# An attention and gated feed-forward kernel: six loads and adds per batch in place of eight accumulating ones

## The chip, the core and the metric

The kernel runs on one core of one Trainium2 chip. The metric is the device time of one execution in microseconds (us), the median of several runs. In the text PE is the engine of the matrix products, DVE the vector engine, ACT the scalar engine, POOL the GpSimd engine, SP the engine that issues most of the DMAs. Each engine works through its own list of instructions in a fixed order and waits where an operand is not ready.

## The reference

Keys and values are averaged over groups of 8 positions, so 576 queries of each of 8 batches and 8 heads meet 72 pooled keys and values; then comes a gated feed-forward layer.

```python
k_p = k.reshape(B, H, Sp, pool, D).mean(axis=3)      # B=8 H=8 S=576 Sp=72 D=64
v_p = v.reshape(B, H, Sp, pool, D).mean(axis=3)
scores = scale * q @ k_p.T; attn = softmax(scores)
x = (attn @ v_p)  # to 4608 rows of 512
g = x @ w_gate                                       # 512 -> 1536
out = (g / (1 + exp(-g)) * (x @ w_val)) @ w_out      # 1536 -> 512
```

All inputs and outputs are float32. The kernel splits each float32 operand into two 16-bit parts and adds up three products, which keeps the precision.

## The kernel before, in words

The 4608 rows of x are nine tiles of 512. A tile is filled by pieces of up to 128 queries, 40 pieces in all, 5 of each batch. A piece (the function `answer`) goes: scores on PE (L578), maximum and subtraction on DVE (L587, L588), exponential on ACT, a high part on ACT (L649) and a low part on POOL (L654, L655), a DMA transpose by SP into the tile `pt` (L1198), products with the values on PE (L663 to L666 for batches 0 and 1, L673 to L679 for batches 2 to 7), division on DVE (L683), a low part of x on POOL (L1315) and, for batches 2 to 7, one more DMA transpose by SP into x (L1319).

The feed-forward layer of a tile is 12 steps, one for each chunk of 128 hidden units. A plain step is 24 products of 512 columns (L775 to L777). A fast step does the same by a scheme of seven half-size products: 42 products of 256 columns (L879), with two additions on DVE (L942, L947); it needs weights that were converted on DVE, POOL and ACT (L800, L806, L812, L819) and sums of x (L840 to L848). Tiles 0 and 1 use plain steps. The gate's end is L723 (ACT) and L726 (DVE), the value's end L731 (DVE), and the result is stored to DRAM (`hd`, L903). From about 737 us on the product with w_out runs (L1565 to L1580).

The weights come as chunks in 64-bit form and are decoded on DVE, ACT and POOL (L335 to L389); the 12 chunks of w_out are loaded and decoded likewise (L330, then L335 and L358 with 512 columns) and stored back to DRAM (L395).

Batches 0 and 1 pool their keys and values on DVE, POOL and PE (L400 to L407, L501). For batches 2 to 7 the host only lays keys and values out as eight parts of 128 x 864 numbers, the eight positions of a group; they are added up while they are loaded: SP loads the first part (L1159), and POOL issues seven DMAs that accumulate onto it (L1161), each after the one before has landed. The sum lies in a buffer called box, one for even and one for odd batches. Then `prep` takes its maximum on DVE (L459), sums it over the rows on PE (L303, L304), scales, and spreads the result on ACT, DVE and POOL (L469 to L481).

What stands in each engine's list, and in which order, is decided at build time by the class Order: a planner in which every piece of work is a generator that asks for buffers, for flags, or for an engine with an assumed duration; the planner always takes what can begin first and, among what can begin nearly at once, the lowest rank. Buffers are handed out from pools: `mid` (3 buffers), `load` (3 tokens for bulk loads of SP), PSUM banks `gate`, `val`, `att`, `vs`. An assumed duration in the source is a number for this planner and not a measurement. A changed duration, pool or rank moves instructions on all engines.

Of the kernel before, what the change touches and what calls it, by code (L numbers as in the profile page):

```python
# [17 lines left out]
P = 128  # L18
POOLW = 8
# [42 lines left out]
class Order:  # L62
# [40 lines left out]
    def flag(self, name):  # L103
        return "flag", name
# [85 lines left out]
def attention_then_swiglu(  # L190
# [90 lines left out]
    )  # L281
    zeros = hp.tile([P, TILE // 2], F32, name="zeros", tag="rs0", bufs=1).bitcast(F16)

# [8 lines left out]
    def fields():  # L292
        nc.gpsimd.memset(zeros, 0.0)
        for i in range(2):
            nc.gpsimd.memset(halves[i][:, 2 * NJ * P :], 0.0)
            nc.gpsimd.memset(vst_h[i], 0.0)
            nc.gpsimd.memset(vst_l[i], 0.0)
# [459 lines left out]
    def f_room(name):  # L757
# [234 lines left out]
    def chunk(c):  # L992
# [25 lines left out]
        tj = t  # L1018
        t = yield op("ACT", 1640, lambda: w_sums(c), tj)
        where, t0 = yield get("att")  # L1020
        t = yield op("PE", 300, lambda: w_total(c, where), t, t0)
        t = yield op("DVE", 350, lambda: w_scale(c), t)
        put("att", where, t)
        order.start(("early", u + 0.01), factors(c, t))
        for i in range(2):
            th = yield op("ACT", 716, lambda: w_high(c, i), t)
            tl = yield op("DVE", 690 + 0 * i, lambda: w_low(c, i), th)
            order.done(("decoded", c, i), tl)

    def factors(c, t):  # L1030
        t = yield op("POOL", 450, lambda: nc.gpsimd.tensor_mul(p2w[:, c, 2:3], p2w[:, c, 0:1], p2w[:, c, 1:2]), t)
# [4 lines left out]
        t = yield op("POOL", 450, lambda: nc.gpsimd.tensor_mul(un_of[0][:, c], p2w[:, c], xs[0]["mt"]), t)  # L1036
        order.done(("un", c), t)
# [37 lines left out]
    def keys(b, g):  # L1075
        if b:
            n, t0 = yield get("mid")
            t = yield bulk(576, lambda: k_load(b, g, n), t0)
            t = yield op("POOL", 2900, lambda: k_sum(b, g), t)
            put("mid", n, t)  # L1080
        else:
            if not g:
                where, t0 = yield get("ws")
            t = yield bulk(576, lambda: k_load(b, g), 0)
            if g:
                tp = yield op("POOL", 1500, k_last, t)
                t = yield op("DVE", 1190, lambda: k_sum(b, g), t)
                t = max(t, tp)
                t = max(t, (yield flag(("keys", 0, 0))))
                spent.append((raw, "raw"))  # L1090
                put("ws", (raw, "raw"), t)
            else:
                t = yield op("DVE", 2210, lambda: k_sum(b, g), t)
        order.done(("keys", b, g), t)

    def pooled_values(b):
# [15 lines left out]
        order.done(("scaled", b), t)  # L1112
        order.start(("early", (0.32, SECOND + 0.32)[b]), left_values(b, t))
# [3 lines left out]
        put(("gate", "val")[b], where, max(t, tl[0]))  # L1117
        order.done(("values", b), max(t, tl[1]))
# [6 lines left out]
    def values_in(b, g, where, t0):  # L1125
# [3 lines left out]
        t = yield bulk(512, lambda: v_load(b, g, n), tm)  # L1129
        t = yield op("PE", 1850, lambda: v_sum(b, g, where), t, t0)  # L1130
        if n is not None:
# [21 lines left out]

    def kv_sums(b, t):
        box(0)
        box(1)
        o = home["kv", b % 2]
        src = kv[b - SPLIT]
        t = yield bulk(400, lambda: nc.sync.dma_start(out=o, in_=src[0]), t)  # L1159
        for n in range(1, POOLW):  # L1160
            t = KV_LAND + (yield op("POOL", 900, lambda: nc.gpsimd.dma_start(out=o, in_=src[n], accum_op=ALU.add), t))  # L1161
        order.done(("kv", b), t)

    def prep(b):

        split = yield flag("boxes")
        if b > SPLIT + 1:
            split = yield flag(("split", b - 2))
        order.start(("kv", b), kv_sums(b, split))
        t = yield flag(("kv", b))  # L1170
        mx = small.tile([P, 1], F32, name="mx1")
# [6 lines left out]

        t = yield op("PE", 300, total, t, t0)
        t = yield op("DVE", 350, lambda: pow2_above(p2s[:, b, 2:3], inv[:, b, 2:3], sums_of["ps"]), t)  # L1180
# [19 lines left out]
    def tile_x(i):  # L1200
# [10 lines left out]

        t = yield op("DVE", 900, rates, t)
        order.done(("rate", i), max(t, t0))
# [11 lines left out]
    def answer(t):  # L1225
# [15 lines left out]
        for g in range(2):  # L1241
            homes[g], t1 = yield get("att")
            t0 = max(t0, t1)
        tp = yield op("PE", 750, lambda: ps.update(scores(b, s0, m, homes)), ta, t0)
        put("qt", t["qt"], tp)
# [5 lines left out]
        if old:  # L1251
# [6 lines left out]
            if t["n"] in ON_POOL:  # L1258
                tp = yield op("POOL", 1560, lambda: normalise(nc.gpsimd, m, sc, t["ri"]), tp)
# [4 lines left out]
            tp = yield op("ACT", 1100, lambda: soft_high(m, sc, half), tp, th)  # L1264
            tp = yield op("POOL", 1700, lambda: soft_low(m, sc, half), tp)
            put("sc", s, tp)
# [13 lines left out]
        if not old:  # L1280
# [4 lines left out]

            te = max(tr, (yield op("DVE", 1030, ratios, te)))
        where, t0 = yield get("att")
        ps = {}
        x = xs[i]
        if old:  # L1290
# [8 lines left out]
            tp = yield op("DVE", 750, lambda: x_low(ps["o"], m, x, off, r), tp)  # L1299
            put("att", where, tp)  # L1300
        else:
# [8 lines left out]
            tp = yield op("DVE", 750, lambda: divided(o, ps["o"], m, t["ri"], r), tp, te)  # L1310
            put("att", where, tp)
            n, t0 = yield get("xt")
# [16 lines left out]
        if not left_of["b", b]:  # L1329
            order.done(("batch", b), tp)  # L1330

    wpart = {}
# [124 lines left out]
    def cut_operand(p, k, src, t):  # L1457
# [3 lines left out]
        for n in range(3):  # L1461
            th = yield op("ACT", 1043, lambda: nc.scalar.copy(rows[n], src[:, 2 * n : 2 * n + 2]), t, t0)  # L1462
            eng, ns, on = (("POOL", 2500, nc.gpsimd), ("DVE", 2000, nc.vector))[n == 2]
            tl = yield op(
# [200 lines left out]
    def all_lines():  # L1665

        home["ws"] = const.tile([P, 3 * 3 * DM // 2], F32, name="mixed", tag="wo_l", bufs=1)
        order.free["DVE"], order.free["POOL"] = 3300, 2400
        order.done("start", 0)

        def first_fields():
            order.done("fields", (yield op("POOL", 2800, fields, 0)))
# [4 lines left out]
        order.start(("early", 0.3), pooled_values(0))  # L1677
        for c in range(NCH):
# [102 lines left out]
```

## Time and profile before

| what | value |
|---|---|
| median of 3 runs | 1008.36 us (1005.07 to 1016.50) |
| profiled execution, its own time | 1008.69 us |
| span from its first to its last instruction | 1006.9 us |
| PE busy | 904.1 us, 90% of the span |
| DVE, ACT, POOL busy | 715.7, 474.5, 509.3 us |
| DMA queue of POOL (accumulating) | 18.58 MB, 12.5% of 16 engines' span |
| DMA queue of SP | 126.84 MB, 45.6% |

The profile is one execution; times in it count from the span's start. A wait is an engine's idle time before an instruction and is put down to what ended it. PE's matmuls overlap, so PE can be called busy while it waits a little; what PE needs at full pace is read from the number of products in a stretch in which it never waits.

### The profile page before, as it was taken

The numbers are of one execution on the slowest core, as the hardware profiler recorded it, in microseconds if no ns is written. First come the engines' busy times: TensorE is split into PE (matmuls) and PEld (weight loads), VectorE is DVE, ScalarE is ACT, GpSimd is POOL, SyncE is SP. The second block draws the span as 40 slices with busy tenths as digits, with TensorE's granted clock in tenths as the row PEclk, the third lists the DMA queues.
The fourth block names the chain that finished last, engine by engine and source line by source line (L and its number), as shares of the span: only waits on it lengthen the run. The fifth ranks groups of instructions, "written<-read, shape, count | busy, mean of one in ns | idle before, by whom it ended". The sixth has DMA issues, their size and how long they took to land. (4 is left out here: it accounts for less than half of the span.)

```text
span 1006.9 us, 17492 instructions
## 1 busy us (share of the span) xinstructions
PE 904.1 (90%) x6708; PEld 641.7 (64%) x6730; DVE 715.7 (71%) x1095; ACT 474.5 (47%) x821; POOL 509.3 (51%) x437
## 2 busy tenths in 40 slices
PE   5579887768699898899999999999999899999998
PEld 4566443333367577688878888888855455555554
DVE  7878693672889788888686765547754959687791
ACT  3776652331354465556454444446544344354442
POOL 2542462554465497636342421203355767778692
PEclk9588997998799999999999999999999999999999
DMA  8935997999888878855445241123653080625301
GB/s 287 303 103 170 237 189 142 191 159 154 140 168 178 155 171 186 187 131 131 93 108 118 70 101 62 61 66 127 220 219 105 8 306 21 253 81 190 145 22 63
DMA packets 136148, 146.54 MB, mean 146 GB/s; under 512 B 81792, under 2 KB 102272, under 8 KB 133760
## 3 DMA queue, kind: packets, MB, share of 16 engines
q1 hardware_dynamic: 130016, 126.84, 45.6%
q0 software_dynamic: 6048, 18.58, 12.5%
q8 instruction: 53, 0.87, 0.4%
q14 instruction: 31, 0.25, 0.1%
HBM read 86.51 MB, written 40.89 MB: 127 GB/s over the span
## 5 line engine op out<-in xcount | busy, mean ns | idle before, releaser
L1579 PE MATMUL ps<-low,wsh 128*128 128x512 bf16 x384 | 146.2, 381 | 5.7 <-DVE low L1466 4.1
L879 PEld LDWEIGHTS <-mixed 128*128 128x128 f16 x1404 | 136.4, 98 | 20.3 <-issue 2.1
L879 PEld LDWEIGHTS <-wgv_h 128*128 128x128 f16 x1248 | 121.0, 98 | 35.6 <-issue 17.1
L723 ACT ACTIVATE hf<-ps,un 128x512 f32<-128x512 f32 (+1 forms) x112 | 75.0, 670 | 104.9 <-PE ps L879 61.8
L879 PE MATMUL ps<-xc,mixed 128*128 128x256 f16 x936 | 123.2, 274 | 0.9 <-ACT ps L939 0.9
L879 PE MATMUL ps<-xc,wgv_h 128*128 128x256 f16 x624 | 110.7, 274 | 14.7 <-DVE ps L947 12.7
L726 DVE SCALAR_TENSOR_TENSOR hf<-hf,ps 128x512 f32<-128x512 f32 (+1 forms) x112 | 74.2, 663 | 64.6 <-ACT hf L723 64.2
L731 DVE SCALAR_TENSOR_TENSOR hf<-ps,un,hf 128x512 f32<-128x512 f32 (+1 forms) x112 | 81.4, 727 | 49.6 <-PE ps L879 28.6
L879 PE MATMUL ps<-x,wgv_h 128*128 128x256 f16 x624 | 109.2, 273 | 0.0
L776 PE MATMUL ps<-x,wgv_h 128*128 128x512 f16 (+1 forms) x272 | 101.7, 374 | 1.2 <-DVE x L693 1.2
L777 PE MATMUL ps<-x,wgv_l 128*128 128x512 f16 (+1 forms) x272 | 101.3, 373 | 1.3 <-DVE wgv_l L389 1.3
L775 PE MATMUL ps<-x,wgv_h 128*128 128x512 f16 (+1 forms) x272 | 102.5, 377 | 0.0
L879 PE MATMUL ps<-xc,wgv_l 128*128 128x256 f16 x312 | 85.6, 274 | 0.0
L879 PE MATMUL ps<-x,wgv_l 128*128 128x256 f16 x312 | 85.0, 273 | 0.0
L1579 PEld LDWEIGHTS <-wsh 128*128 128x128 bf16 x384 | 37.5, 98 | 50.9 <-issue 9.5
L1161 POOL DMA_DIRECT2D box<-kv_parts x42 | 37.1, 899 | 63.0 <-DMA box<-kv_parts 61.2
L1466 POOL TENSOR_TENSOR low<-wgv_h,hs 128x1024 bf16<-128x1024 f32 x18 | 51.2, 2868 | 33.7 <-ACT hs L1462 33.7
L1315 POOL TENSOR_TENSOR box<-sc,box 128x512 f16<-128x512 f32 (+1 forms) x30 | 38.5, 1284 | 54.4 <-ACT box L1314 54.4
L879 PEld LDWEIGHTS <-wgv_l 128*128 128x128 f16 x624 | 61.2, 98 | 7.4
L879 PE MATMUL ps<-x,mixed 128*128 128x256 f16 x468 | 64.5, 274 | 0.5 <-DVE ps L942 0.5
L654 POOL TENSOR_TENSOR half<-sc,half 128x448 f16<-128x448 f32 (+1 forms) x30 | 33.4, 1114 | 55.8 <-ACT half L649 55.6
L844 POOL TENSOR_TENSOR fx<-fx 128x256 f32<-128x256 f32 x40 | 29.6, 740 | 60.1 <-DVE fx L840 57.8
(181 smaller groups left out, 2101.4 us busy)
## 6 DMA issues: line engine op xcount, KB each, us to landing
hd<-hf SPq DMA_DIRECT2D x104, 256.0 KB, 2.4
ws<-w_all SPq DMA_DIRECT2D x36, 512.0 KB, 6.0
box<-kv_parts POOLq DMA_DIRECT2D x42, 432.0 KB, 7.7
wgv_h<-hd SPq DMA_DIRECT2D x9, 1536.0 KB, 6.8
wgv_l<-hd SPq DMA_DIRECT2D x9, 1536.0 KB, 8.9
out_t<-ob SPq DMA_DIRECT2D x36, 256.0 KB, 4.1
qt<-q_rows SPq DMA_DIRECT2D x32, 256.0 KB, 3.9
wd<-wf SPq DMA_DIRECT2D x12, 256.0 KB, 4.3
```

Of the source, the lines that this page charges most:

```text
L654: nc.gpsimd.tensor_sub(a[:, :, SP:], sc[:n, :, : P - SP], a[:, :, : P - SP])
L723: nc.scalar.activation(hf, gate, AF.Tanh, scale=un[:, c, 0:1])
L726: nc.vector.scalar_tensor_tensor(out=hf, in0=hf, scalar=1.0, in1=gate, op0=ALU.add, op1=ALU.mult)
L731: nc.vector.scalar_tensor_tensor(out=out, in0=val, scalar=un[:, c, 2:3], in1=hf, op0=ALU.mult, op1=ALU.mult)
L775: nc.tensor.matmul(o, wh, x["h"][:, j, a:e], start=(j == 0), stop=False)
L776: nc.tensor.matmul(o, wh, x["l"][:, j, a:e], start=False, stop=False)
L777: nc.tensor.matmul(o, wl, x["h"][:, j, a:e], start=False, stop=(j == NJ - 1))
L879: nc.tensor.matmul(o, a, b, start=begin and j + n == 0, stop=j == HJ - 1 and n == 2, skip_group_check=True,)
L1161: t = KV_LAND + (yield op("POOL", 900, lambda: nc.gpsimd.dma_start(out=o, in_=src[n], accum_op=ALU.add), t))
L1315: tp = yield op("POOL", 1205, lambda: nc.gpsimd.tensor_sub(xt[:, DM:], o, xt[:, :DM]), tp)
L1466: lambda: on.tensor_sub(low[:, 2 * n : 2 * n + 2], src[:, 2 * n : 2 * n + 2], rows[n].bitcast(F32)),
L1579: nc.tensor.matmul(o, top, where[1][:, c], start=False, stop=False, skip_group_check=True)
```

## The change

It has four parts.

1. Keys and values of batches 2 to 7: the accumulating DMAs go. A batch is loaded in six parts, each with all eight positions of 144 of the 864 columns (128 x 8 x 144, 576 KB, one contiguous row of 4608 bytes in each partition). SP issues the load into a buffer of `mid`, and POOL adds the eight up with three additions (576, 288 and 144 numbers a partition) into box. 6 loads and 42 accumulating DMAs become 36 loads and 36 groups of three additions.
2. PSUM: the products of values for batches 0 and 1 get a bank of their own (`wv`, formerly one of two banks of `val`), and both banks of `vs` go to `val` later; after batch 1 the bank `wv` is lent to `gate`.
3. The rank of the first values (0.9 in place of 0.3) and the assumed durations of several operations change, and the first operations stand in another order.
4. A buffer of zeros that nothing reads is no longer cleared.

```diff
-KV_LAND = 5500
+BANKS = "val", "val"
+VALUES = 0.9
+LENT = "gate"
...
-            "gate": [(ps_gv, "gv0"), acc[0]], "val": [(ps_gv, "gv1"), acc[1]], "vs": [acc[2], acc[3]],
+            "gate": [(ps_gv, "gv0"), acc[0]], "val": [(ps_gv, "gv1")], "wv": [acc[1]], "vs": [acc[2], acc[3]],
...
-    def kv_sums(b, t):
-        o = home["kv", b % 2]
-        src = kv[b - SPLIT]
-        t = yield bulk(400, lambda: nc.sync.dma_start(out=o, in_=src[0]), t)
-        for n in range(1, POOLW):
-            t = KV_LAND + (yield op("POOL", 900, lambda: nc.gpsimd.dma_start(out=o, in_=src[n], accum_op=ALU.add), t))
-        order.done(("kv", b), t)
+    def kv_part(b, c, ready):
+        n, t0 = yield get("mid")
+        _, t1 = yield get("load")
+        part = {}
+        def load():
+            part["in"] = buffer(mid, [P, POOLW, KV // 6], F32, "in", "mid", at=n)
+            nc.sync.dma_start(out=part["in"], in_=kv[b - SPLIT, c])
+        t = yield bulk(576, load, t0, t1)
+        cs = slice(c * KV // 6, (c + 1) * KV // 6)
+        dst = home["kv", b % 2][:, cs]
+        def add():
+            a = part["in"]
+            nc.gpsimd.tensor_add(a[:, :4], a[:, :4], a[:, 4:])
+            nc.gpsimd.tensor_add(a[:, :2], a[:, :2], a[:, 2:4])
+            nc.gpsimd.tensor_add(dst, a[:, 0], a[:, 1])
+        t = yield op("POOL", 2800, add, t, ready)
+        put("mid", n, t)
+        order.done(("kv", b, c), t)
...
-            order.start(("early", (0.31, SECOND + 0.3)[b] + 0.01 * g), values_in(b, g, where, max(t, tb)))
+            order.start(("early", (VALUES, SECOND + 0.3)[b] + 0.01 * g), values_in(b, g, where, max(t, tb)))
...
-        where, t0 = yield get("att")
+        where, t0 = yield get("wv" if old else "att")
...
+            if b == SPLIT - 1:
+                where, t0 = yield get("wv")
+                put(LENT, where, t0)
...
+    kv = kv.reshape(B - SPLIT, POOLW, P, 6, -1).transpose(0, 3, 2, 1, 4)
```

The first place is POOL's list where batches 2 and 3 are spread (L473) and the first low parts of their weights are made (L654, L655). Before, it reads (box is the buffer with the sums, fw a buffer for converted weights, half the low parts of a piece):

```order
L473 TENSOR_TENSOR box<-box,masks 128x512 x2
L1161 DMA box<-kv_parts 128x864
L654 TENSOR_TENSOR half_135<-sc,half_135 128x8x56
L655 TENSOR_TENSOR half_135<-sc,half_135 128x128
L806 TENSOR_TENSOR fw<-fw 128x256 x2
L1161 DMA box<-kv_parts 128x864 x2
L806 TENSOR_TENSOR fw<-fw 128x256 x2
L654 TENSOR_TENSOR half_136<-sc,half_136 128x8x56
L655 TENSOR_TENSOR half_136<-sc,half_136 128x128
```

Now it reads (in is the loaded part):

```order
L473 TENSOR_TENSOR box<-box,masks 128x512
L1169 TENSOR_TENSOR in<-in 128x576
L1170 TENSOR_TENSOR in<-in 128x288
L1171 TENSOR_TENSOR box<-in 128x144
L1169 TENSOR_TENSOR in<-in 128x576
L1170 TENSOR_TENSOR in<-in 128x288
L1171 TENSOR_TENSOR box<-in 128x144
L654 TENSOR_TENSOR half_135<-sc,half_135 128x8x56
L655 TENSOR_TENSOR half_135<-sc,half_135 128x128
L1169 TENSOR_TENSOR in<-in 128x576
L1170 TENSOR_TENSOR in<-in 128x288
L1171 TENSOR_TENSOR box<-in 128x144
```

Additions stand where accumulating DMAs were issued, and two groups of them stand in front of the first low part; batch 3 is spread later, after batch 2's first two pieces have passed POOL.

The second place is SP's list where the first two pieces of batch 2 are transposed (pt and x are the transposes' targets, qt the queries, hd the stored results, ws and wd chunks of w_out). Before:

```order
L330 DMA ws<-w_all 128x1024
L1159 DMA box<-kv_parts 128x864
L562 DMA qt<-q_rows 128x4x128
L903 DMA hd<-hf 128x512
L1198 DMA_TRANSPOSE pt<-half_135 128x9x128
L903 DMA hd<-hf 128x512
L1198 DMA_TRANSPOSE pt<-half_136 128x9x128
L1319 DMA_TRANSPOSE x<-box 128x8x128
```

Now:

```order
L330 DMA ws<-w_all 128x1024
L562 DMA qt<-q_rows 128x4x128
L1216 DMA_TRANSPOSE pt<-half_135 128x9x128
L1161 DMA in<-kv_parts 128x1152
L903 DMA hd<-hf 128x512
L1216 DMA_TRANSPOSE pt<-half_136 128x9x128
L1161 DMA in<-kv_parts 128x1152
L903 DMA hd<-hf 128x512
L395 DMA wd<-wf_1626 128x512
L1337 DMA_TRANSPOSE x<-box 128x8x128
```

Loads of parts stand between the transposes, and each of them must wait until POOL has added up an earlier part and so freed a buffer of `mid`. This is also the first load of a w_out chunk; before, it was the third.

Over the whole program PE has 912 products of plain steps in place of 816 and 3108 of fast steps in place of 3276, that is four steps that were fast and are plain. Ahead of the last of the 24 instructions that finish the weights (L389) DVE has 228 instructions in place of 223. POOL has 8 of the 36 groups of additions ahead of the last chunk's factors (L1036), and before it had 10 of the 42 accumulating DMAs there.

## Rows read from the trace of the kernel before

**Rows 1.** Busy time, granted clock and DMA share by stretch; the columns stand above.

```profile
core 0: us, PE busy (x) PEld busy (x) DVE busy (x) ACT busy (x) POOL busy (x), PEclk, DMA share, GB/s
0.00:50.00 50.00, 26.05 (x187) 24.69 (x188) 41.42 (x73) 26.86 (x44) 21.86 (x39) 0.76 0.96 294
...
147.00:300.00 153.00, 116.95 (x738) 61.69 (x737) 93.64 (x170) 49.71 (x81) 72.89 (x85) 0.89 0.97 161
300.00:425.00 125.00, 111.12 (x1020) 87.15 (x1019) 105.91 (x182) 69.13 (x127) 86.08 (x98) 0.96 0.84 174
425.00:737.00 312.00, 305.86 (x3017) 268.31 (x3016) 214.87 (x411) 156.41 (x325) 105.47 (x108) 1.00 0.40 108
```

**Rows 2.** PE's waits between 147 and 300 us: total us, times, longest.

```profile
PE ps L673 <- DMA pt<-half: 19.7, 4, 11.2
PE ps L578 <- DVE sc L588: 9.0, 1, 9.0
PE ps L304 <- DVE mx L459: 4.5, 1, 4.5
```

**Rows 3.** PE's waits between 300 and 425 us.

```profile
PE ps L879 <- DVE ps L947: 8.0, 5, 3.7
PE ps L673 <- DMA pt<-half: 3.9, 1, 3.9
```

**Rows 4.** DMAs between 185 and 262 us: count, KB each, median us to landing.

```profile
q0 software_dynamic: 1655, 5.11, 52.1%
...
box<-kv_parts POOLq DMA_DIRECT2D x12, 432.0 KB, 9.7
...
pt<-half SPq DMA_TRANSPOSE x4, 10.9
x<-box SPq DMA_TRANSPOSE x4, 15.9
```

**Rows 5.** DMAs between 425 and 560 us.

```profile
pt<-half SPq DMA_TRANSPOSE x12, 3.5
```

**Rows 6.** Idle time of POOL before L1161, by what ended it: us, times.

```profile
  DMA box<-kv_parts: 61.2, 22
```

**Rows 7.** POOL between 147 and 425 us, groups: busy us, mean ns | idle.

```profile
L1161 POOL DMA_DIRECT2D box<-kv_parts x32 | 28.0, 885 | 43.9 <-DMA box<-kv_parts 42.1 <-DVE hf L726 1.5 <-issue 0.3
L806 POOL TENSOR_TENSOR room<-room 128x256 f32<-128x256 f32 x24 | 23.1, 963 | 3.1 <-DVE room L800 2.5
```

**Rows 8.** Additions on POOL, by line: ns min/median/max, first and last start, forms.

```profile
L625 POOL TENSOR_TENSOR sc<-sc,ri x7: 1142/1151/1589, 61.3 to 148.7; 128x576 f32<-128x576 f32 x5, 64x576 f32<-64x576 f32 x2
...
L405 POOL TENSOR_TENSOR kr<-kr x2: 1403/1870/2337, 31.4 to 36.8; 128x576 f32<-128x576 f32 x2
L405 POOL TENSOR_TENSOR k<-k x1: 789/789/789, 6.2 to 6.2; 128x288 f32<-128x288 f32 x1
...
L406 POOL TENSOR_TENSOR kr<-kr x2: 1122/1393/1664, 33.8 to 38.2; 128x288 f32<-128x288 f32 x2
L406 POOL TENSOR_TENSOR k<-k x1: 487/487/487, 7.1 to 7.1; 128x144 f32<-128x144 f32 x1
...
L407 POOL TENSOR_TENSOR spare<-kr x2: 821/854/887, 35.6 to 39.4; 128x144 f32<-128x144 f32 x2
```

**Rows 9.** Three short stretches, columns as in Rows 1.

```profile
350.00:375.00 25.00, 24.57 (x221) 18.33 (x220) 21.70 (x37) 16.02 (x30) 20.99 (x23) 0.95 0.70 173
625.00:650.00 25.00, 25.00 (x230) 22.29 (x228) 13.04 (x24) 11.46 (x24) 9.88 (x12) 1.00 0.15 54
241.00:254.00 13.00, 13.00 (x62) 5.91 (x61) 4.26 (x9) 1.34 (x2) 4.38 (x6) 1.00 1.32 119
```

**Rows 10.** L335 on DVE: one instruction in the timeline, then the whole line.

```profile
404.75 5.63 DVE L335 TENSOR_SCALAR ws<-ws 128x512 uint32<-128x512 uint32 x1
...
L335 DVE TENSOR_SCALAR ws<-ws x24: 408/686/5626, 19.2 to 422.9; 128x1024 uint32<-128x1024 uint32 x12, 128x512 uint32<-128x512 uint32 x12
```

More of the change, by code (lines that the diff above doesn't have):

```diff
@@ L1078, in keys @@
             t = yield bulk(576, lambda: k_load(b, g, n), t0)
-            t = yield op("POOL", 2900, lambda: k_sum(b, g), t)
+            t = yield op("POOL", 3800, lambda: k_sum(b, g), t)
             put("mid", n, t)
@@ L1116, in pooled_values @@
         tl = yield flag(("left", b))
-        put(("gate", "val")[b], where, max(t, tl[0]))
+        put(BANKS[b], where, max(t, tl[0]))
         order.done(("values", b), max(t, tl[1]))
@@ L1129, in values_in @@
         t = yield bulk(512, lambda: v_load(b, g, n), tm)
-        t = yield op("PE", 1850, lambda: v_sum(b, g, where), t, t0)
+        t = yield op("PE", 2300, lambda: v_sum(b, g, where), t, t0)
         if n is not None:
@@ L1168, in prep @@
             split = yield flag(("split", b - 2))
-        order.start(("kv", b), kv_sums(b, split))
-        t = yield flag(("kv", b))
+        box(0)
+        box(1)
+        t = 0
+        for c in range(6):
+            order.start(("kv", b + 0.1 * c), kv_part(b, c, split))
+        for c in range(6):
+            t = max(t, (yield flag(("kv", b, c))))
         mx = small.tile([P, 1], F32, name="mx1")
@@ L1210, in rates @@
             rate[i] = scales(bs, xs[i]["mt"])
-        t = yield op("DVE", 900, rates, t)
+        t = yield op("DVE", 1300, rates, t)
         order.done(("rate", i), max(t, t0))
@@ L1258, in answer @@
             if t["n"] in ON_POOL:
-                tp = yield op("POOL", 1560, lambda: normalise(nc.gpsimd, m, sc, t["ri"]), tp)
+                tp = yield op("POOL", 1300, lambda: normalise(nc.gpsimd, m, sc, t["ri"]), tp)
             else:
@@ L1263, in answer @@
             half = halves[h]
-            tp = yield op("ACT", 1100, lambda: soft_high(m, sc, half), tp, th)
-            tp = yield op("POOL", 1700, lambda: soft_low(m, sc, half), tp)
+            tp = yield op("ACT", 910, lambda: soft_high(m, sc, half), tp, th)
+            tp = yield op("POOL", 1950, lambda: soft_low(m, sc, half), tp)
             put("sc", s, tp)
@@ L1299, in answer @@
             tp = yield op("DVE", 750, lambda: x_low(ps["o"], m, x, off, r), tp)
-            put("att", where, tp)
+            put("wv" if old else "att", where, tp)
         else:
@@ L1310, in answer @@
             tp = yield op("DVE", 750, lambda: divided(o, ps["o"], m, t["ri"], r), tp, te)
-            put("att", where, tp)
+            put("wv" if old else "att", where, tp)
             n, t0 = yield get("xt")
@@ L1462, in cut_operand @@
             th = yield op("ACT", 1043, lambda: nc.scalar.copy(rows[n], src[:, 2 * n : 2 * n + 2]), t, t0)
-            eng, ns, on = (("POOL", 2500, nc.gpsimd), ("DVE", 2000, nc.vector))[n == 2]
+            eng, ns, on = (("POOL", 3000, nc.gpsimd), ("DVE", 2000, nc.vector))[n == 2]
             tl = yield op(
@@ L1667, in all_lines @@
         home["ws"] = const.tile([P, 3 * 3 * DM // 2], F32, name="mixed", tag="wo_l", bufs=1)
-        order.free["DVE"], order.free["POOL"] = 3300, 2400
+        order.free["DVE"], order.free["POOL"] = 4000, 1600
         order.done("start", 0)
         def first_fields():
-            order.done("fields", (yield op("POOL", 2800, fields, 0)))
+            order.done("fields", (yield op("POOL", 2700, fields, 8000)))
         for g in range(2):
@@ L1676, in all_lines @@
         order.start(("early", 0.05), first_fields())
-        order.start(("early", 0.3), pooled_values(0))
+        order.start(("early", VALUES), pooled_values(0))
         for c in range(NCH):
```

24 lines of the change are left out of this document (10 added, 14 removed).

## The prediction

> **What bounds the kernel now.** I first read the busy shares by stretch [rows 1]. From 425 to 737 us PE is busy 305.9 of 312 us at full clock: nothing but less work shortens that stretch. Between 147 and 300 us it is busy only 117 of 153, at a granted clock of 0.89, while no other engine is full (DVE 93.6, POOL 72.9). So this stretch is bound by waits between engines, and the change is worth what it does there. Next come the waits of PE in it [rows 2]: 19.7 us for the transposed weights `pt` of pieces (L673), 9.0 at the scores (L578), 4.5 at the row total of a batch's maximum (L304, behind L459). Then the DMAs, to see why `pt` is late [rows 4, 5]. From 185 to 262 us the accumulating queue alone takes 52.1% of the 16 DMA engines for 5.11 MB, and a transpose lands 10.9 us (`pt`) or 15.9 us (x) after its issue. Once that queue is nearly silent, from 425 us on, the same `pt` transpose lands in 3.5 us. The mean DMA share of 0.97 [rows 1] says the same. Last, POOL: it stands idle 61.2 us behind accumulating DMAs that have not landed [rows 6], with the low parts of pieces queued behind them.
>
> **The change part by part.** I work against the profiled execution's own 1008.7 us; the median of the runs shown, 1008.4, is the same, so nothing is shifted.
>
> *Waits that go.* The accumulating DMAs vanish from the stretch. The four waits on `pt` in rows 2 are at most 11.2 us each, and a transpose there is late by 10.9 - 3.5 = 7.4 us in the median: I let all 19.7 go. The 4.5 us at L304 are the last accumulation of batch 2 landing; seven in a row, at 9.7 us each [rows 4], become loads that do not follow one another, and the total of batch 2 stands three plain steps earlier in PE's list, so it goes as well. The 9.0 us at L578 wait for DVE, which sat behind an x transpose (15.9 us median, [rows 4]); I let it go too. From 300 to 425 us the 3.9 us on `pt` [rows 3] have the same cause. Together 19.7 + 9.0 + 4.5 + 3.9 = 37.1 us. The 8.0 us at L879 there wait for DVE and stay.
>
> *Steps that were fast and are plain.* Four. A fast step at full pace is 42 x 25.0 / 230 us = 4.57 us, a plain one 24 x 13.0 / 62 us = 5.03 us [rows 9]: +1.9 us, all of it on PE.
>
> *The additions on POOL.* 36 groups of 576 + 288 + 144 numbers. No row shows them on these tiles. From below: 1.14 us (L625, 576 numbers, shortest) + 0.79 (L405, 288) + 0.49 (L406, 144) = 2.42 us a group. From above: the two groups of the same size on kr, 1.40 + 1.12 + 0.89 = 3.41 and 2.34 + 1.66 + 0.82 = 4.82 us, both made in the opening [rows 8]. Between 147 and 425 us a short addition of the same kind (L806) takes 963 ns in the mean [rows 7] against about 0.7 alone; other lines there are stretched less. I take 1.2 times the lower bound, 2.9 us.
>
> Whether they cost PE anything is a matter of POOL's room. From 147 to 425 us POOL is busy 72.9 + 86.1 = 159.0 of 278 us [rows 1]. The issues take 28.0 of it and go [rows 7]; 28 groups stand behind the last chunk's factors, and I put all of them into the stretch: 28 x 2.9 = 81.2. That makes 159.0 - 28.0 + 81.2 = 212.2 us of work. Without any hindrance the stretch would shrink to 278 - 37.1 + 1.9 = 242.8 us, and POOL would be busy 87% of it. The busiest 25 us that POOL has in this half are 20.99, or 84% [rows 9]. Taking that as the most that a fixed order lets through, the stretch needs 212.2 / 0.84 = 252.6 us: +9.8 us against 242.8.
>
> *The rest.* The loads of parts move the bytes of the old ones in plain DMAs of SP; a plain 512 KB load of the same queue in the opening is no wait of PE here, so they count nothing as long as SP isn't held up (second rival). SP's list is passed by them at 36 places. The w_out decoding (L330, L335, L358) moves behind, its first load from third to first at the place shown; DVE has 312 - 214.9 = 97 idle us from 425 to 737 us [rows 1], so it costs nothing there. The opening up to 147 us is full of DVE work (41.4 of the first 50 us, [rows 1]) and ends with the weights' last split. DVE has 228 instructions before it in place of 223: I take 0, with 6 us to either side for the values that load later and the earlier first steps. PSUM: `gate` has one bank less and `val` one more until batch 1 is done; PE waits for no bank in rows 2, so 0. Clearing the zeros: 0, POOL idles then.
>
> *Sum:* 1008.7 - 37.1 + 1.9 + 9.8 = 983.3 us.
>
> **The rivals.**
>
> *POOL and DVE hold each other up, and the kernel gets slower.* On DVE a short instruction (L335, 512 numbers) took 5.63 us at 404.75 us, while POOL worked without a pause; the line's shortest is 408 ns [rows 10]. More additions mean more such runs, and the additions get longer too: on kr they took 3.41 and 4.82 us while DVE was busy 83% [rows 1, 8]. At their mean, 4.1, POOL's work is 131.0 + 114.8 = 245.8, and the stretch 245.8 / 0.84 = 292.6 us: 1008.7 + 14.6 = 1023 us. It decides from (278 x 0.84 - 131.0) / 28 = 3.66 us a group on, where the stretch gets no shorter at all. For it: DVE will be just as busy here, 199.5 of about 250 us. Against it: much of DVE's work in this stretch reads PSUM (L731, L726, L588), and L806 was stretched by a third and not doubled. Chance 0.14.
> The Trainium skill, SBUF — State Buffer, section "SBUF: two separate sides", says that GpSimd and VectorE share one pair of ports and that it is "an exclusive lock, not a bandwidth split": one of them stops for the whole of the other's instruction, when VectorE reads two SBUF inputs or runs in a two-port mode. By that rule the additions take the ports for all of their time, and it speaks for this rival; the 5.63 us of L335 agree with it; by the rule the sum is the 1023 us above, by the mean stretch of L806 the 983.
>
> *SP is held up.* A load of a part must wait until POOL has freed a buffer of `mid`, and behind it in SP's list stand the transposes of pieces. If POOL is late by a few us at each, the transposes are late again, now by their issue and not by their landing. With half of the 37.1 us back: 983.3 + 18.6 = 1002 us. For it: three buffers, and loads between nearly all transposes of batches 2 to 4. Against it: POOL's list has the additions ahead of the low parts that the same transposes wait for anyway. Chance 0.2.
>
> *POOL costs nothing and DVE's waits go too.* If groups take 2.42 us, POOL's 131.0 + 67.8 = 198.8 us fit (198.8 / 0.84 = 237, under 242.8). The 8.0 us at L879 [rows 3] came when L335 of w_out stood in DVE's list before L947, and that work is moved out of the way. Then 1008.7 - 37.1 - 8.0 + 1.9 = 965.5 us. Chance 0.15.
>
> *The DMA engines were not the cause:* transposes stay at 10 us beside plain loads too, and only the 4.5 us at L304 go: about 1008.7 - 4.5 + 1.9 + 9.8 = 1016 us. Rows 4 and 5 speak against it, since the stored results and the queries go on in both. Chance 0.03.
>
> **How the numbers follow.** My forecast, 983 us, has a chance of 0.48; with groups of 2.42 to 3.41 us and 6 us for the opening it runs from 970 to 1000. The 80% range, 964 to 1010, takes in the better rival and the case of SP, and leaves out most of the two slow cases. A measurement of this kernel can tell about 1% (10 us) from no change, so faster means below 998 us. Faster: nearly all of the forecast (0.46), the better rival (0.15), and a quarter of the SP case (0.05): 0.66. Slower by over 1%: most of POOL against DVE (0.11) and a part of the last rival (0.01): 0.12. Within 1%: the remaining 0.22.
>
> **What would show it.** In the new profile the median landing of `pt` transposes between 150 and 260 us should be below 5 us, and PE's waits on `pt` at L673 there below 8 us in total. The groups of additions (L1169 to L1171) should take 2.4 to 3.4 us; above 3.7 us the forecast is wrong on that term. POOL should be busy over 75% between 147 and 400 us. The product with w_out should begin at about 737 - 25 = 712 us, and take 270 us as before. Waits of SP's queue at L1161 with late transposes behind them would show the second rival; DVE's mean of L335, L840 and L848 above twice their shortest would show the first.

## The result and the profile after

The changed kernel takes 962.76 us (median of 4 runs, 958.7 to 966.16), the kernel before 1006.72 us (4 runs, 998.1 to 1016.5). The ratio is 0.9589 with a 95% interval of 0.9512 to 0.9667: faster by 4.1%. The kernel before has a slower run among its four that the ratio leaves out, so it is not the quotient of the two medians. Forecast were 983 us with a range of 964 to 1010. The direction was right, and the gain some 1.7 times what was forecast (44 us in place of 25). The median lies 1 us below the range; on the 1008.4 us that the prediction worked against, the ratio gives 967 us.

The profiled execution of the changed kernel took 958.7 us, with a span of 956.9 us. Its busy time by stretch, with the columns of [rows 1], reads:

```profile
core 0: us, PE busy (x) PEld busy (x) DVE busy (x) ACT busy (x) POOL busy (x), PEclk, DMA share, GB/s
0.00:50.00 50.00, 33.62 (x260) 31.58 (x261) 39.96 (x85) 27.78 (x49) 22.13 (x40) 0.86 0.96 313
147.00:300.00 153.00, 141.81 (x1012) 79.40 (x1011) 126.77 (x216) 61.56 (x102) 130.46 (x141) 0.99 0.71 180
300.00:425.00 125.00, 117.01 (x1101) 93.86 (x1100) 99.69 (x176) 67.84 (x130) 97.58 (x109) 0.99 0.57 150
425.00:687.00 262.00, 257.96 (x2511) 226.59 (x2509) 178.26 (x338) 138.78 (x281) 83.42 (x82) 1.00 0.43 118
687.00:956.90 269.90, 259.46 (x1134) 143.79 (x1154) 182.70 (x113) 109.14 (x128) 179.14 (x61) 0.99 0.36 130
```

Between 147 and 300 us PE now makes 1012 products where it made 738, at a granted clock of 0.99 in place of 0.89. POOL went from 72.9 to 130.5 busy us of 153, DVE from 93.6 to 126.8. The product with w_out begins at 687 us (before at 737) and takes 270 us as it did. So the whole gain is made ahead of it.

PE's waits between 147 and 300 us, the largest and those that answer to [rows 2], in total us, times, longest:

```profile
PE ps L673 <- DMA pt<-half: 3.3, 4, 1.4
...
PE ps L578 <- DVE sc L588: 0.3, 1, 0.3
```

and the one between 300 and 425 us that answers to [rows 3]:

```profile
PE ps L879 <- DVE ps L947: 5.2, 6, 2.0
```

The three waits of [rows 2] were 33.2 us. They are 3.6 us now; the wait at L304 is gone. All waits of PE that the trace lists in this stretch sum to 11.0 us in place of 35.9. The DMAs between 185 and 262 us, the stretch of [rows 4]:

```profile
in<-kv_parts SPq DMA_DIRECT2D x11, 576.0 KB, 5.3
...
x<-box SPq DMA_TRANSPOSE x6, 3.6
pt<-half SPq DMA_TRANSPOSE x5, 4.0
```

In the median the transposes land in 3.6 and 4.0 us where they took 15.9 and 10.9, as the prediction had it (below 5). SP's own issue of them got shorter too. Here is the line of these transposes in the kernel before and then in the changed one (ns min/median/max of the issue):

```profile
L1198 SPq DMA_TRANSPOSE pt<-half x40: 1202/1425/10603, 21.2 to 587.6; - x40
```

```profile
L1216 SPq DMA_TRANSPOSE pt<-half x40: 1212/1323/2614, 16.5 to 538.5; - x40
```

Before, one issue held SP for 10.6 us, and everything behind it in SP's list waited as long.

The table shows when PE had finished a given number of steps, counted from its products (24 of a plain or 42 of a fast step make one; eight of the first are half as wide, 256 columns). It is used below, in us, for kernels that the next section explains:

```
step               8      16     24     32     56     108
before            94.6  153.2  233.4  297.8  451.0  714.9
changed           78.6  142.1  201.2  253.2  402.0  665.8
rest only         80.4  144.5  208.6  281.0  432.0  695.7
parts only        94.3  152.0  206.4  260.8  402.0  666.5
parts, 1 addition 95.1  153.4  205.4  255.8  392.4  657.8
changed, 1 add.   79.0  135.5  189.5  238.3  378.0  641.7
more additions    79.5  154.6  219.4  281.0  446.3  710.1
plain writes      94.3  154.0  228.3  280.5  423.2  687.0
POOL issues loads 95.0  163.1  224.2  282.8  425.4  691.2
```

The changed kernel is 11 us ahead after 16 steps, 49 us after 56, and keeps that to the end.

### The profile page after: what moved, and what is told of

Its sections match the earlier page's. It is cut to its first block, busy times and chain, and to the rows that moved or that the text cites. A ratio compares the mean times of both kernels' runs of the same rounds, so it can differ in the third digit from the quotient of the medians.

```text
span 956.9 us, 17399 instructions
## 1 busy us (share of the span) xinstructions
PE 895.9 (94%) x6636; PEld 629.2 (66%) x6658; DVE 717.6 (75%) x1087; ACT 468.9 (49%) x809; POOL 580.4 (61%) x502
## 3 DMA queue, kind: packets, MB, share of 16 engines
q1 hardware_dynamic: 134336, 145.42, 51.7%
## 5 line engine op out<-in xcount | busy, mean ns | idle before, releaser
L879 PEld LDWEIGHTS <-mixed 128*128 128x128 f16 x1332 | 129.2, 98 | 23.4 <-issue 5.6
L879 PEld LDWEIGHTS <-wgv_h 128*128 128x128 f16 x1184 | 114.3, 98 | 33.2 <-issue 15.1
L879 PE MATMUL ps<-xc,mixed 128*128 128x256 f16 x888 | 118.2, 274 | 3.5 <-ACT ps L939 3.5
L879 PE MATMUL ps<-xc,wgv_h 128*128 128x256 f16 x592 | 104.8, 273 | 9.3 <-DVE ps L947 7.7
L777 PE MATMUL ps<-x,wgv_l 128*128 128x512 f16 (+1 forms) x304 | 110.5, 364 | 2.6 <-DVE wgv_l L389 2.6
L775 PE MATMUL ps<-x,wgv_h 128*128 128x512 f16 (+1 forms) x304 | 110.7, 364 | 0.4 <-ACT wgv_h L384 0.4
L776 PE MATMUL ps<-x,wgv_h 128*128 128x512 f16 (+1 forms) x304 | 110.6, 364 | 0.0
L731 DVE SCALAR_TENSOR_TENSOR hf<-ps,un,hf 128x512 f32<-128x512 f32 (+1 forms) x112 | 81.2, 726 | 34.3 <-PE ps L879 27.6
L879 PE MATMUL ps<-x,wgv_h 128*128 128x256 f16 x592 | 103.6, 273 | 2.5 <-ACT rs L937 2.4
L1487 POOL TENSOR_TENSOR low<-wgv_h,hs 128x1024 bf16<-128x1024 f32 x18 | 51.2, 2867 | 33.2 <-ACT hs L1483 33.2
L1487 POOL TENSOR_TENSOR low<-wgv_h,more 128x1024 bf16<-128x1024 f32 x16 | 47.2, 2972 | 24.3 <-ACT more L1483 24.3
L1169 POOL TENSOR_TENSOR in<-in 128x576 f32<-128x576 f32 x36 | 55.4, 1540 | 7.8 <-DMA in<-kv_parts 5.7
L1601 PE MATMUL ps<-hs,wsl 128*128 128x512 bf16 x148 | 57.2, 387 | 0.0
```

The lines of the kernel that those rows point to most:

```text
L731: nc.vector.scalar_tensor_tensor(out=out, in0=val, scalar=un[:, c, 2:3], in1=hf, op0=ALU.mult, op1=ALU.mult)
L775: nc.tensor.matmul(o, wh, x["h"][:, j, a:e], start=(j == 0), stop=False)
L776: nc.tensor.matmul(o, wh, x["l"][:, j, a:e], start=False, stop=False)
L777: nc.tensor.matmul(o, wl, x["h"][:, j, a:e], start=False, stop=(j == NJ - 1))
L879: nc.tensor.matmul(o, a, b, start=begin and j + n == 0, stop=j == HJ - 1 and n == 2, skip_group_check=True,)
L1169: nc.gpsimd.tensor_add(a[:, :4], a[:, :4], a[:, 4:])
```

## The experiments

Three sets of four kernels were run, each set on one chip beside runs of the kernel before. That kernel scatters (1000 to 1028 us in the first set), the others by 1.3% and less. Each kernel is given with its ratio to the kernel before in the same set and its interval; kernels without accumulating DMAs are also compared by their medians, across chips where they are of different sets.

**The parts alone.** The edit puts the first part of the change into the kernel before, and nothing else:

```diff
+        for c in range(6):
+            order.start(("kv", b + 0.1 * c), kv_part(b, c, split))
-        order.start(("kv", b), kv_sums(b, split))
...
+    kv = kv.reshape(B - SPLIT, POOLW, P, 6, -1).transpose(0, 3, 2, 1, 4)
```

> The kernel before with the first part of the change alone (six plain loads and additions per batch; PSUM banks, ranks, assumed durations and first operations as before). In the changed kernel the PE is 11 us ahead after 16 steps and 49 us ahead from step 56 on. Theory: the 38 us between come from the accumulating DMAs that are gone, the 11 us from the other parts; then this kernel takes about 1007 - 38 = 969 us, with the first 16 steps no earlier than before. Rival, the accumulating DMAs slowed the opening too: about 960 us, with step 16 some 10 us early. Rival, the gain is the other list order and not the DMAs: 990 us or more.

Measured: 961.3 us, ratio 0.9504 (0.9446 to 0.9562). The parts alone give all that the change gives, 8 us more than the theory's 969 us allowed. The first rival named the right time with the wrong cause: the first 16 steps end at 152.0 us, no earlier than before, and yet PE is level with the changed kernel at step 56 (402.0 in both). So the 11 us of the opening are not added to the rest; something takes them back on the way.

**The rest alone.** The changed kernel with the accumulating DMAs put back:

```diff
-            order.start(("kv", b + 0.1 * c), kv_part(b, c, split))
+        order.start(("kv", b), kv_sums(b, split))
```

> The changed kernel with the accumulating DMAs put back (all other parts of the change kept). Theory: only the opening's 11 us remain, so about 996 us, with transposes of pt landing about 10 us after issue between 185 and 262 us. Rival, the opening gained because the accumulating DMAs went: about 1007 us. Rival, the list order made the gain: about 970 us.

Measured: 989.1 us, ratio 0.977 (0.9712 to 0.9828), 7 us under the 996 of the theory. The other parts are worth 17 to 29 us of 1007 where the accumulation stays; 9 us of that are there after 16 steps and 19 after 56. But the waits stay with the accumulation. Between 147 and 300 us (lines past L46 stand one further down in this kernel):

```profile
PE ps L674 <- DMA pt<-half: 18.7, 4, 12.4
PE ps L305 <- DVE mx L460: 11.0, 1, 11.0
```

These were 19.7 and 4.5 us in the kernel before, so the new order of the lists does not take them away. The 9.0 us at L578 are gone here all the same (0.2 us are left at that line). The two halves of the change, 46 and some 20 us, together give 44: they don't add up.

**More additions.** In the changed kernel the first addition of each group is made twice, the lists otherwise the same:

```diff
             nc.gpsimd.tensor_add(a[:, :4], a[:, :4], a[:, 4:])
+            nc.gpsimd.tensor_add(a[:, :4], a[:, :4], a[:, 4:])
```

> The changed kernel with the first of the three additions of each group made twice (the sums are then not the reference's), in the same list order. A group should take about 1.4 us more, 4.5 us in the mean. By the room that the prediction gave POOL (84% of the stretch, 28 groups), the kernel gets 28 x 1.4 / 0.84 = 47 us slower: about 1010 us. If POOL has no such ceiling and only its late results count, it gets slower by 5 to 20 us: 968 to 983 us. If POOL was not near any limit: within 3 us of 963.

Measured: 1005.6 us, 43 us more than the changed kernel; against the kernel before the ratio is 0.998 (0.9944 to 1.0017), no difference. POOL's own lines, from 85 to 400 us (busy us, mean ns | idle before), give 165.9 us of additions:

```profile
L1170 POOL TENSOR_TENSOR in<-in 128x576 f32<-128x576 f32 x36 | 57.2, 1589 | 2.8
L1169 POOL TENSOR_TENSOR in<-in 128x576 f32<-128x576 f32 x36 | 52.5, 1458 | 4.5 <-DMA in<-kv_parts 2.7 <-issue 1.7
L1171 POOL TENSOR_TENSOR in<-in 128x288 f32<-128x288 f32 x36 | 33.9, 940 | 2.8
L1172 POOL TENSOR_TENSOR box<-in 128x144 f32<-128x144 f32 x36 | 22.3, 620 | 2.8
```

The changed kernel has 114.2 us of them in the same stretch:

```profile
L1169 POOL TENSOR_TENSOR in<-in 128x576 f32<-128x576 f32 x36 | 55.4, 1540 | 7.8 <-DMA in<-kv_parts 5.7 <-PE ps L578 1.9
L1170 POOL TENSOR_TENSOR in<-in 128x288 f32<-128x288 f32 x36 | 35.4, 984 | 2.8
L1171 POOL TENSOR_TENSOR box<-in 128x144 f32<-128x144 f32 x36 | 23.4, 649 | 2.8
```

So 51.7 us more of POOL's work cost 43 us of time, 0.83 of each us. The changed kernel stands where POOL's work is paid for nearly in full, and with a group of 4.6 us (165.9 us for 36) the whole gain is gone.

**Fewer additions.** The other direction: the changed kernel with the last addition of each group only.

```diff
-            nc.gpsimd.tensor_add(a[:, :4], a[:, :4], a[:, 4:])
-            nc.gpsimd.tensor_add(a[:, :2], a[:, :2], a[:, 2:4])
             nc.gpsimd.tensor_add(dst, a[:, 0], a[:, 1])
```

> The changed kernel with only the last of the three additions of each group (most of the sums left out), in the same list order; POOL has 28 x 2.5 = 70 us less to do between 147 and 425 us. By the prediction's term the additions cost 9.8 us there, so about 953 us. If POOL does not bound the stretch: within 3 us of 963. If additions and DVE hold each other up much: 945 us or less, with DVE instructions shorter.

Measured: 939.3 us, 23.4 us less than the changed kernel; ratio 0.9294 (0.9226 to 0.9362). Of the 114.2 us of additions 21.8 us are left, so 92.4 us of POOL's work gave back 23.4 us, 0.25 of each us. The lowest theory (945 or less) came out right on the time, but not on its cause: DVE, 123.0 us for 221 instructions between 147 and 300 us, takes 557 ns for one where it took 587 (126.8 for 216), only 5% less in the mean of all its instructions. PE no longer waits for anything long there:

```profile
147.00:300.00 153.00, 150.88 (x1134) 89.58 (x1132) 123.02 (x221) 67.47 (x114) 91.68 (x112) 1.00 0.77 200
```

```profile
PE ps L879 <- DVE hf L731: 0.7, 1, 0.7
PE ps L673 <- DMA pt<-half: 0.6, 1, 0.6
```

The first row is the stretch by engine, the others are PE's longest waits in it: PE is busy 150.9 of 153 us at a clock of 1.00.

**The parts alone, with fewer additions.** This tells what becomes of the opening's lead.

```diff
+            order.start(("kv", b + 0.1 * c), kv_part(b, c, split))
...
+            nc.gpsimd.tensor_add(dst, a[:, 0], a[:, 1])
```

> The kernel before with the first part of the change alone, and only the last of the three additions of each group (sums left out). With all additions it took 961 us though its first 16 steps end 10 us later than in the changed kernel. Theory: POOL's list hides that difference; with POOL relieved it comes back, so this kernel is 8 to 16 us slower than the changed one with fewer additions (939): 947 to 955 us. Rival, the opening's lead is worth nothing anyway: about 939 us.

Measured: 952.9 us, ratio 0.9484 (0.9416 to 0.9552), 13.6 us over the changed kernel with fewer additions. The theory stands: with POOL relieved, the opening's lead is worth 14 us; with all additions, nothing (961.3 against 962.8). The parts-only kernel shows why in its stretch row:

```profile
147.00:300.00 153.00, 144.62 (x1080) 83.20 (x1079) 128.80 (x219) 62.10 (x103) 141.40 (x151) 1.00 0.69 186
```

POOL is busy 141.4 of 153 us. My reading is that with POOL that full, a PE that arrives earlier waits the longer for what POOL hands on. The runs show only that the lead comes back when POOL is relieved.

**What makes the opening's lead.** Both kernels are the changed one with fewer additions, the first with all assumed durations and first operations as before, the second with the PSUM banks as before:

```diff
-        t = yield op("ACT", 1240, lambda: w_sums(c), tj)
+        t = yield op("ACT", 1640, lambda: w_sums(c), tj)
...
-        order.free["DVE"], order.free["POOL"] = 4000, 1600
+        order.free["DVE"], order.free["POOL"] = 3300, 2400
```

> The changed kernel with only the last addition of each group (939 us), with all assumed durations and the start of the first operations as before; PSUM banks and the rank of the values as changed. The opening's lead is worth 14 us there. If the durations and the order of the first operations make it: 949 us or more, with step 8 ending at about 94 us. If the PSUM bank makes it: within 4 us of 939.

```diff
-            "gate": [(ps_gv, "gv0"), acc[0]], "val": [(ps_gv, "gv1")], "wv": [acc[1]], "vs": [acc[2], acc[3]],
+            "gate": [(ps_gv, "gv0"), acc[0]], "val": [(ps_gv, "gv1"), acc[1]], "vs": [acc[2], acc[3]],
```

> The same kernel (939 us) with only the PSUM banks as before (no bank of its own for the early value products, nothing lent). If the bank makes the opening's lead of 14 us: 949 us or more, with step 8 ending at about 94 us. If durations and order make it: within 4 us of 939. Both apart may also cost half of it each.

Measured: 944.8 us (ratio 0.9371, 0.9302 to 0.9439) and 948.1 us (0.9409, 0.9328 to 0.949), that is 5.5 and 8.8 us over 939.3. By the medians each has a share, 14.3 us together. But the sets ran on different chips, and the intervals, some 7 us to either side, overlap with that of the kernel at 939.3 us: the shares are not shown beyond the noise, nor which is the larger. Neither brings step 8 back to 94 us, as was expected of the one that makes the lead (82.0 and 82.8 us); most of the loss comes between steps 8 and 16 (step 16 ends at 145.7 and 146.6 us against 135.5). The rank of the first values and the zeros were not tried alone.

**Plain writes in place of accumulation.** The kernel before, with one word less:

```diff
-nc.gpsimd.dma_start(out=o, in_=src[n], accum_op=ALU.add)
+nc.gpsimd.dma_start(out=o, in_=src[n])
```

> The kernel before with its 42 DMAs of POOL as plain writes over the buffer, without accumulation (the sums are left out), same list order, same bytes, each still behind the one before. Theory: the accumulating packets fill the DMA engines, so plain ones let a transpose of pt land in 3 to 5 us between 185 and 262 us, and the kernel gets 35 to 60 us faster: 950 to 975 us. Rival, the chain of seven landings per batch and not the kind of packet holds things up: the transposes stay above 8 us and the time within 10 us of before.

Measured: 985.2 us, ratio 0.9818 (0.9719 to 0.9918), 8 to 28 us faster than before: neither theory's time. In the median the transposes do land sooner, as the first theory said, but by the medians only 22 us come with it, less than half of what the parts alone gain (46). Between 185 and 262 us, queue and landings:

```profile
q0 software_dynamic: 1040, 5.75, 29.4%
...
box<-kv_parts POOLq DMA_DIRECT2D x12, 432.0 KB, 5.1
...
pt<-half SPq DMA_TRANSPOSE x5, 4.7
x<-box SPq DMA_TRANSPOSE x4, 4.6
```

More bytes than in [rows 4] (5.75 MB against 5.11) take 29.4% of the DMA engines in place of 52.1%. But PE still waits 13.5 us for `pt` between 147 and 300 us, where it waited 19.7:

```profile
PE ps L673 <- DMA pt<-half: 13.5, 3, 8.0
```

The medians hide why. Here are the `pt` transposes of the whole execution (L1198), in the kernel before and then with plain writes:

```profile
DMA to landing us min/median/max: 2.8/4.1/15.0
```

```profile
DMA to landing us min/median/max: 2.8/4.1/14.0
```

PE's two longest waits for `pt` in this run, 8.0 and 4.4 us, end as a transpose lands that took 14.0 and one that took 9.6 us.

**The loads issued by POOL.** The kernel with the parts alone and one addition, its plain loads moved from SP's list to POOL's:

```diff
-            nc.sync.dma_start(out=part["in"], in_=kv[b - SPLIT, c])
+            nc.gpsimd.dma_start(out=part["in"], in_=kv[b - SPLIT, c])
```

> The run with the first part of the change alone and only the last addition of each group (953 us), its 36 plain loads now issued by POOL, the other engines' lists unchanged. POOL gets 36 issues of some 0.6 us, 20 us of work, and its additions stand close behind a load that has not landed. The kernel before with plain writes kept about 30 us of loss that the packets' kind doesn't explain. Theory: that loss is POOL's list waiting for landings, with the low parts behind; then this run is 15 to 35 us slower, 968 to 988 us. Rival, it came only from seven writes that follow one another onto one buffer: within 5 us of 953.

Measured: 982.6 us, ratio 0.9742 (0.9654 to 0.983), 30 us slower than with SP's loads (952.9). So plain DMAs that POOL issues are dear here, without any chain of writes onto one buffer. The reason that the theory gave for it finds no support: POOL stands idle 17.3 us behind loads that have not landed, and in the kernel with SP's loads 26.5 us, without harm. Ten of the 30 us are lost before step 16 ends. Between 147 and 300 us the clock is at 0.92, and `pt` comes late:

```profile
147.00:300.00 153.00, 136.96 (x925) 74.54 (x923) 111.95 (x202) 55.81 (x97) 86.86 (x115) 0.92 0.69 169
```

```profile
PE ps L673 <- DMA pt<-half: 8.2, 2, 6.4
```

What is late are again single transposes. Here are the `pt` transposes of this kernel (L1214), and then of the one with SP's loads:

```profile
DMA to landing us min/median/max: 2.8/3.8/11.6
```

```profile
DMA to landing us min/median/max: 2.9/3.6/6.3
```

The wait of 6.4 us ends as the one of 11.6 us lands. I counted in every trace the transposes (of `pt` and x) between 100 and 420 us that landed more than 8 us after their issue: 9 in the kernel before and 8 with the rest alone, 6 with plain writes, 3 here. Every one of these 26 had DMAs of POOL in flight beside it. In the ten kernels whose loads SP issues there is none. So a DMA that POOL issues, plain or accumulating, can make a transpose beside it late. Why it does, and what else makes up the 30 us, stays open.

**Some groups on DVE.** One, two or three of a batch's six parts are summed by one reduction on DVE in place of three additions on POOL:

```diff
+        def reduce():
+            nc.vector.tensor_reduce(out=dst, in_=part["in"].rearrange("p w k -> p k w"), axis=AX.X, op=ALU.add)
+        if c in (2, 5):
+            t = yield op("DVE", 1400, reduce, t, ready)
```

> The changed kernel with one part of six of each batch summed by a single reduction on DVE in place of the three additions on POOL. POOL has 6 x 3.1 = 19 us less, DVE about 6 x 1.5 = 9 us more. If POOL bounds the stretch with the slope of the run with more additions (43 us for 36 x 1.5 = 54 us, 0.8), up to 15 us faster, by the slope of the run with fewer (24 us for 36 x 2.5 = 90 us, 0.27) 5 us: 948 to 958 us. If DVE, busy 127 of 153 us, is as near its limit: 963 us or more.

> The same with two parts of six on DVE: POOL has 37 us less, DVE 18 us more, so DVE would be busy about 140 of 150 us. If POOL alone bounds: 938 to 953 us. If DVE becomes the bound: slower than with one part of six, 955 to 975 us.

> The changed kernel with three of six parts summed by a reduction on DVE. With two DVE was busy 141 of 153 us between 147 and 300 us, POOL 120. If DVE is now the bound, slower than with two: 955 us or more. If the two engines can still trade: 940 to 950 us.

Measured: 961.6 us with one (ratio 0.9568, 0.9518 to 0.9617), **951.6 us** with two (0.9478, 0.9421 to 0.9534), 964.7 us with three (0.9575, 0.9505 to 0.9646). Two of six is the fastest complete kernel here, 11 us under the changed one. One part gave nothing that can be measured, less than expected, and its list order differs as well. A reduction takes 2.1 us, not the 1.5 that was expected. The stretches with two, and then with three:

```profile
147.00:300.00 153.00, 143.97 (x1069) 86.67 (x1069) 140.91 (x222) 63.08 (x108) 120.40 (x129) 0.99 0.66 173
```

```profile
147.00:300.00 153.00, 140.38 (x1028) 83.22 (x1027) 143.12 (x225) 59.31 (x102) 99.16 (x107) 0.94 0.65 171
```

With two DVE is busy 140.9 us, POOL 120.4. With three POOL falls to 99.2 us, DVE is at 143.1, and PE makes 41 products fewer. By these rows DVE is the bound then; no run relieves it alone.

## Why the prediction was right, and what it mis-sized

**The waits that go: they were named right; their price was not, and their cause only in part.** Of the 37.1 us, nearly all went as told: `pt` 19.7 to 3.3, L578 9.0 to 0.3, L304 4.5 to nothing. The cleanest price is the kernel with the parts alone and one addition, which leaves the opening as it was: between step 16 and step 56 it takes 239.0 us where the kernel before takes 297.8. So 58.8 us went, where the sum has 36.2 (37.1 less 0.9, since two of the four steps are plain in this kernel). The failed step is that the sum took PE's idle time for the whole cost of its waits. What it left out is in [rows 1], the granted clock of 0.89, which the prediction read and then priced at nothing. The kernel before around its longest wait shows it:

```profile
218.50:221.00 2.50, 0.00 (x0) 0.00 (x0) 2.01 (x3) 2.50 (x5) 1.87 (x2) 1.00 1.47 64
221.00:225.00 4.00, 0.00 (x0) 0.00 (x0) 1.83 (x5) 0.09 (x1) 0.00 (x0) 0.74 1.29 177
225.00:230.00 5.00, 0.37 (x1) 0.13 (x2) 0.00 (x0) 0.00 (x0) 2.69 (x4) 0.50 0.96 186
229.80:235.40 5.60, 5.59 (x32) 2.54 (x30) 0.75 (x1) 0.85 (x2) 3.80 (x6) 0.70 1.24 165
```

PE stands still from 218.4 to 229.6 us; the granted clock falls from 1.00 to 0.50 (the level of 1.2 GHz) and is at 0.70 in the mean over the 5.6 us that follow. The first product after the wait shows the price in its own length:

```profile
229.63 0.61 PE L673 MATMUL ps<-box,pt 128*128 128x512 f16 x1 [11.22 <-DMA pt<-half]
```

It takes 0.61 us where the line's median is 0.379. I compared each product's distance to the next with the median for its shape (over four of the kernels), from step 16 to step 56. The kernel before loses 49.0 us in gaps over 0.5 us and 11.8 in smaller excess; the kernel with the parts alone and one addition 4.8 and -1.1. So 44 us of the difference are gaps, 7 more than the 37.1 of the sum, since waits that were to stay shrank too. The other 13 us are slow products, which no wait in the lists carries. They lie where the clock was low: over these steps it was granted at the level of 1.2 GHz for 44 us in the kernel before, and never in the other. At that level two products of 512 columns stood 426 ns apart in the median, at 2.4 GHz 216, and the products begun at the lower level hold all of the smaller excess (14.2 us; the others -2.4).

As to the cause, the prediction laid the late transposes to accumulating packets that fill the DMA engines. The run with plain writes keeps 13.5 of the 19.7 us at L673. By the medians the accumulation makes 22 us (1007 to 985.2), and POOL as the issuer of plain DMAs 30 (982.6 to 952.9); together that is about the 54 that went. So the larger part comes with SP as the issuer, which the prediction passed over. And that late x transposes made the 9.0 us at L578 is not shown: with the rest alone they go while the accumulation stays.

**The additions.** A group was set at 2.9 us. Between 147 and 425 us the three lines read:

```profile
L1169 POOL TENSOR_TENSOR in<-in 128x576 f32<-128x576 f32 x26 | 39.0, 1499 | 5.8 <-DMA in<-kv_parts 5.7
L1170 POOL TENSOR_TENSOR in<-in 128x288 f32<-128x288 f32 x26 | 25.5, 981 | 2.0
L1171 POOL TENSOR_TENSOR box<-in 128x144 f32<-128x144 f32 x26 | 16.7, 641 | 2.0
```

That is 1.50 + 0.98 + 0.64 = 3.12 us a group, for 26 groups in place of 28: 81.2 us, the very sum of the prediction. Its price, 9.8 us, is met by the kernels with parts alone (961.3 against 952.9 with one addition, so 8.4 us for two of the three additions). In the changed kernel it is 23.4 us, because there the additions also take back the lead of the opening. The rule behind the 9.8 held POOL to 84% of its stretch. Between 147 and 400 us the changed kernel has it busy 213.9 of 253 us, 85%, but that is no ceiling: 88% in the parts-only kernel, 92% with more additions. As a slope it did well: 43 us measured where it gave 47.

**The opening.** It was put at 0, with 6 us to either side. At step 16 the gain is 11.1 us, so the place was misjudged; at the end the parts that make it are worth nothing (962.8 against 961.3), since the additions take the lead back. That the value 0 came out is luck: the prediction had no such reason.

**The sum again**, by the path of the runs: the medians go from 1007 before to 952.9 (accumulation gone, one addition), to 961.3 (all additions), to 962.8 (the other parts): -54, +8, +1, where the prediction had -35, +10 and 0. On this path one term was mis-sized, the first. In another order the terms are others: 989.1 (the other parts first), 939.3 (accumulation gone, one addition), 962.8 (all additions), that is -18, -50, +23. The first term is too small on both; the small prices of the additions and of the other parts hold only where the accumulation goes first. The 1.9 us for the four steps was not tried alone. Of the prediction's signs, POOL's share, the additions and the waits for `pt` came as told; the product with w_out began at 687 us and not at 712.

**The rivals.** POOL and DVE holding each other up to 1023 us did not come. DVE took 587 ns for an instruction between 147 and 300 us, 551 before, and by the sign that was set, means above twice the shortest, it did not show: L840 takes 1580 ns in the mean and 1186 at the least, L848 on DVE 958 and 633. Single cases exist: this L840, while POOL worked on low parts and additions, took three times its shortest:

```profile
199.62 3.56 DVE L840 TENSOR_TENSOR fx<-x 128x1024 f32<-128x1024 f16 x1
```

By the exclusive lock that the Trainium skill describes (SBUF — State Buffer, "SBUF: two separate sides") such cases are to be expected. In sum DVE's instructions got 5% shorter when most of the additions went, and an addition's median is at its minimum (1406 against 1390 ns for L1169). The rival's threshold was too low: the gain was to be gone from some 3.7 us a group on. At 3.12 us it is 44 us and at 4.6 it is gone, so in between, by an even slope, some 27 us would be left at 3.7. SP held up by POOL: SP waited for POOL at L1161 20.3 us from 100 to 400 us, 4.5 of them from 147 us on, and PE's waits for `pt` in the latter stretch are short (3.3 us). POOL free: refuted by the run with fewer additions, though its time, 965.5, is the nearest to the result; the wait at L947 that it let go is still 5.2 us. DMA engines not the cause: refuted by the landings.

## What to carry to other kernels

Where PE waits in many places, the idle time in the list of waits is not their whole price: the granted clock of the stretch tells how much slower the products behind them ran, and that time comes back as well. When a change takes a bound away, look at the engine that is to do the work instead, and price its next us: here 0.25 us of time for one us of work less, 0.83 for one more. And two gains on one path need not add: a lead in front of a full engine is lost in it. A median of landing times can hide what an engine waits for: look at the longest, and at what was in flight beside it.

## What the runs showed of the hardware

- By its packets' time, an accumulating DMA took twice the DMA engines' time per byte of a plain one: 52.1% of 77 us for 5.11 MB [rows 4], 7.9 us per MB, against 29.4% for 5.75 MB, 3.9 us per MB. Over the whole execution the same 18.58 MB took 12.5% and 6.8%, a ratio of 1.9. The Trainium skill (Collectives: The Full Stack, section "The bandwidth ceiling: the fold count and why AG ≠ RS ≠ AR") names the cause for sums between cores: the add needs two source reads. The ratio of 2.0 agrees; that it is the cause here no run shows.
- Beside DMAs that POOL issued, a transpose of SP landed as late as 17.4 us (accumulating), 14.0 and 11.6 us (plain) after its issue, and its issue alone held SP up to 10.6, 5.6 and 4.5 us. In the ten kernels whose loads SP issues, no transpose took over 8.0 us to land or 3.9 us to issue.
- Plain loads of the same bytes cost 30 us more when POOL issued them than when SP did, with most of POOL's work otherwise taken away.
